# Pooled and local attention before a SoLU feed-forward layer: a shorter conversion of the float64 weights, g taken in where w_out is rounded, and the first batch's pooled q and k formed by matmuls, in a new order of the program

## The chip, the core and the metric

The kernel runs on one core of one Trainium2 chip. The metric is the device time of one execution, in microseconds (us). Before the change three runs gave 586.81, 589.69 and 590.03 us, median 589.69.

## What is computed

The inputs are q, k and v of 8 batches, 8 heads, 576 tokens and 64 dimensions in float32, two weight matrices w_in (512 x 1024) and w_out (1024 x 512) in float64, and a vector g. Per batch and head there are two attentions, whose results are added:

```
q_d = q.reshape(B, H, Sd, factor, D).mean(axis=3)      # factor 4; k_d and v_d alike
out_up = np.repeat(sm_attn(q_d, k_d, v_d), factor, axis=2)
mask = np.abs(pos[:, None] - pos[None, :]) < factor
scores = np.where(mask, scale * q @ k.T, -1000000000.0)
out_local = softmax(scores) @ v
x = (out_up + out_local)                               # as 4608 tokens x 512
h = x @ w_in
solu = h * softmax(h)
ln = (solu - mu) / np.sqrt(var + 1e-06) * g_ln
out = ln @ w_out
```

## The kernel before

**Engines.** PE is the matrix engine, DVE, ACT and POOL are the vector, scalar and general engines, and SP starts the transfers. Every engine works through its own queue in order.

**Feed-forward tiles.** There are 36 tiles of 128 tokens. Every operand of the two big products is split into a rounded high part and the rest (`xh`, `xl`; `wi_h`, `wi_l`; `uh`, `ul`; `wo_h`, `wo_l`), and a product takes three matmuls for each piece: 24 matmuls make `h` (L862) and 24 make `o` (L986). `h` has one buffer in PSUM. The next tile's `h` can start only when the DVE has read the last one twice, for its maximum (`nmx`, L870) and for the product h*exp(h) (L877), with ACT's exp (L874) between. The product, centred, goes out to DRAM and comes back as `v`, is transposed by the DVE (L963) and split into `uh` and `ul` for `o`. So a tile's `o` comes several tiles after its `h`.

**Weights.** The two matrices arrive as 16 pieces of 128 x 512 float64 numbers (0 to 7 of w_in, 8 to 15 of w_out), each seen as pairs of 32-bit words. `f32` makes float32 of a piece in five steps: ACT takes the absolute value of the high word as a float (L364), the DVE or POOL clamps it (L366), the DVE shifts it left by 3 and masks it (L370), the DVE puts sign and top exponent bit in (L375), and the DVE puts the top three bits of the low word in (L379). `piece` then rounds it to the high part on ACT (L410), after a multiplication by g on ACT for w_out (L409), and POOL or the DVE subtracts (L412). All of w_in has to be there before the first `h`.

**Attention of a batch.** For the first two batches (`EarlyBatch`) the tokens lie six to a partition, and PE transposes them: per pair of heads 12 matmuls for q and 12 for k against an identity (L557), into `qp` and `kp` in PSUM, from where ACT or the DVE copies them to `qT` and `kT` (L263 and L265). The DVE then adds groups of four tokens (L419) into `qd_flat` and `kd`. From these come pooled scores (`sd`, L788), their maximum (`mxd`, L795), exp (`pd`, L803), a transpose (`pdt`), and the product with pooled v (`po`). Local attention works on windows of 64 tokens: scores `sc` (L607), for the first two batches on top of a mask added by PE (L600), maximum `mxl` (L620), difference `pl` (L622), exp, sum `sml` (L639), a transpose `plt`, and the product `xp`. Later batches are transposed by the DVE. In the first batch `kp` and the odd `sd` and `sc` use the two banks that later hold `h` (`ps_h`); the others rotate through two buffers (`ps_a`).

**Fillers.** `keep_clock` puts pairs of bfloat16 matmuls whose result nobody reads (`warm`, L1043) on PE, 24 pairs in all.

**The order.** The program is first written down as a list of some 2,000 steps. `ORDER`, a table of step numbers, sets in which order they are given out, and so the order within each engine's queue, SP's transfers among them. `OTHER` lists the steps that use the second of two possible engines. Queues, buffers and semaphores then decide when each runs.

Of the kernel before, what the change touches and what calls it, by code (L numbers as in the profile page):

```python
# [10 lines left out]
F32 = mybir.dt.float32  # L11
F32R = mybir.dt.float32r
I32 = mybir.dt.int32
BF16 = mybir.dt.bfloat16
# [6 lines left out]
F64_LO = struct.unpack("<f", struct.pack("<I", 0x38000000))[0]  # L21
F64_HI = struct.unpack("<f", struct.pack("<I", 0x47EFFFFF))[0]

# [114 lines left out]
def pooled_local_attention_then_solu_ffn(  # L138
# [10 lines left out]
    nc = tc.nc  # L149
# [1006 lines left out]
```

## Time and profile before

The profiled execution took 585.0 us itself, 583.2 us of it from its first to its last instruction (the span). That is below all three timed runs.

| | before |
|---|---|
| time, median of 3 runs | 589.69 us (586.81 to 590.03) |
| profiled execution, own time | 585.0 us |
| its span | 583.2 us |
| TensorE clock granted | 0.999 |
| ACT busy | 333.8 us (57%) |
| POOL busy | 299.5 us (51%) |

The profile gives for each engine the time in which it had an instruction running. A matmul's record reaches to its modelled end, so a row of dependent short matmuls looks busy although PE does little in it; the starts of instructions tell more there. In rows of the timeline the first number is the start in us from the span's beginning, the second the length of the stretch, the word after it the engine, then line, operation, output and inputs, shape and count. A bracket gives idle time of the engine ahead of it and who ended it.

### The profile page before, as it was taken

The numbers are of one execution on the slowest core, as the hardware profiler recorded it, in microseconds if no ns is written. First come the engines' busy times: TensorE is split into PE (matmuls) and PEld (weight loads), VectorE is DVE, ScalarE is ACT, GpSimd is POOL, SyncE is SP. The second block draws the span as 40 slices with busy tenths as digits, with TensorE's granted clock in tenths as the row PEclk, the third lists the DMA queues.
The fourth block names the chain that finished last, engine by engine and source line by source line (L and its number), as shares of the span: only waits on it lengthen the run. The fifth ranks groups of instructions, "written<-read, shape, count | busy, mean of one in ns | idle before, by whom it ended". The sixth has DMA issues, their size and how long they took to land.

```text
span 583.2 us, 15261 instructions
## 1 busy us (share of the span) xinstructions
PE 564.1 (97%) x5852; PEld 434.1 (74%) x5852; DVE 469.3 (80%) x779; ACT 333.8 (57%) x750; POOL 299.5 (51%) x447
## 2 busy tenths in 40 slices
PE   7899998999999999999999999999999999999996
PEld 3676666777787777877777777777787777788875
DVE  7989999898988879998977967899878877545541
ACT  4778678468546646565565753466445654444442
POOL 3657677957454745648533546356433752334120
PEclk9999999999999999999999999999999999999999
DMA  8997767787877888876867976766755145304230
GB/s 280 286 213 187 189 148 193 200 193 171 228 160 185 188 191 169 194 198 157 208 153 195 228 190 167 212 157 159 195 163 148 56 145 164 127 36 163 90 110 37
DMA packets 207113, 99.59 MB, mean 171 GB/s; under 512 B 163136, under 2 KB 193344, under 8 KB 207040
## 3 DMA queue, kind: packets, MB, share of 16 engines
q1 hardware_dynamic: 207040, 98.61, 66.3%
q8 instruction: 46, 0.75, 0.6%
q14 instruction: 27, 0.22, 0.1%
HBM read 65.54 MB, written 27.79 MB: 160 GB/s over the span
## 4 chain that ended last, share of the span: by engine, by line
PE 64%; DVE 14%; SPq 7%; DMA 5%; ACT 4%; issue 3%; POOL 2%; POOLq 0%; DVEq 0%
PE o L986 27%; PE h L862 25%; SPq L286 4%; DMA v<-u 3%; PE po L844 2%; PE sd L788 2%; PE xp L753 1%; PE pdt L823 1%; PE sc L607 1%; PE sc L695 1%; DVE w L375 1%; DVE qd_flat L419 1%; DVE nmx L870 1%; SPq L942 1%; DVE e L877 1%
## 5 line engine op out<-in xcount | busy, mean ns | idle before, releaser
L986 PE MATMUL o<-wo_h,uh 128*128 128x512 f32 x288 | 116.6, 405 | 1.5 <-ACT osb L993 0.8
L862 PE MATMUL h<-wi_h,xh 128*128 128x512 f32 x288 | 116.9, 406 | 0.8 <-DVE e L877 0.6
L862 PE MATMUL h<-wi_h,xl 128*128 128x512 f32 x288 | 114.1, 396 | 0.7 <-POOL xl L1020 0.7
L986 PE MATMUL o<-wo_l,uh 128*128 128x512 f32 x288 | 113.8, 395 | 0.0
L862 PE MATMUL h<-wi_l,xh 128*128 128x512 f32 x288 | 113.7, 395 | 0.0
L986 PE MATMUL o<-wo_h,ul 128*128 128x512 f32 x288 | 78.9, 395 | 0.0
L972 POOL TENSOR_TENSOR ul<-v,uh 128x512 fp32r<-128x512 f32 x40 | 51.9, 1297 | 42.8 <-ACT uh L969 41.6
L874 ACT ACTIVATE e<-h,nmx 128x1024 f32<-128x1024 f32 x36 | 40.2, 1116 | 49.1 <-DVE nmx L870 45.5
L986 PEld LDWEIGHTS o<-wo_h,uh 128*128 128x128 f32 x288 | 54.0, 188 | 16.8 <-ACT osb L993 1.5
L862 PEld LDWEIGHTS h<-wi_h,xh 128*128 128x128 f32 x288 | 54.1, 188 | 15.8 <-issue 2.9
L862 PEld LDWEIGHTS h<-wi_h,xl 128*128 128x128 f32 x288 | 54.1, 188 | 15.4 <-POOL xl L1020 2.1
L986 PEld LDWEIGHTS o<-wo_h,ul 128*128 128x128 f32 x288 | 54.0, 188 | 13.4 <-DVE ul L972 0.3
L870 DVE TENSOR_REDUCE nmx<-h 128x1 f32<-128x1024 f32 x36 | 43.8, 1216 | 24.2 <-PE h L862 24.2
L986 PEld LDWEIGHTS o<-wo_l,uh 128*128 128x128 f32 x288 | 54.1, 188 | 12.0
L862 PEld LDWEIGHTS h<-wi_l,xh 128*128 128x128 f32 x288 | 54.1, 188 | 11.9
L877 DVE SCALAR_TENSOR_TENSOR e<-h,e 128x1024 f32<-128x1024 f32 x36 | 43.8, 1217 | 14.2 <-ACT e L874 14.0
L969 ACT ACTIVATE uh<-v 128x512 fp32r<-128x512 f32 x70 | 42.9, 624 | 18.5 <-issue 7.1
L963 DVE STREAM_TRANSPOSE v<-v 128x512 f32<-128x512 f32 x70 | 46.4, 689 | 7.6 <-DMA v<-u 7.5
L993 ACT ACTIVATE osb<-o,s 128x512 f32<-128x512 f32 x36 | 24.6, 682 | 40.0 <-PE o L986 22.1
L1020 POOL TENSOR_TENSOR xl<-x,xh 128x512 fp32r<-128x512 f32 (+1 forms) x26 | 32.9, 1268 | 22.5 <-ACT xh L1017 22.2
L487 POOL TENSOR_TENSOR vs<-vs 72x512 f32<-72x512 f32 x24 | 31.9, 1328 | 17.5 <-DMA vs<-in_v_dram 9.0
L882 POOL TENSOR_SCALAR nmu<-su 128x1 f32<-128x1 f32 x36 | 8.1, 226 | 60.1 <-DVE e L877 57.2
(128 smaller groups left out, 1116.3 us busy)
## 6 DMA issues: line engine op xcount, KB each, us to landing
u<-e SPq DMA_DIRECT2D x35, 512.0 KB
v<-u SPq DMA_DIRECT2D x140, 128.0 KB
vs<-in_v_dram SPq DMA_DIRECT2D x32, 288.0 KB
out_dram<-osb SPq DMA_DIRECT2D x36, 256.0 KB
qm<-in_q_dram SPq DMA_DIRECT2D x96, 72.0 KB
km<-in_k_dram SPq DMA_DIRECT2D x96, 72.0 KB
vw<-in_v_dram SPq DMA_DIRECT2D x80, 64.0 KB
vw<-in_v_dram SPq DMA_DIRECT2D x40, 128.0 KB
```

What stands on the lines that cost most here:

```text
L286: nc.sync.dma_start(t[nm][Q * 32:Q * 32 + 32, pr], src[b, 2 * pr + par, :, dh * 32:dh * 32 + 32].rearrange("(k t) d -> t k d", t=32),)
L487: eng.tensor_tensor(out=vs[:, :, 0:2 * D], in0=vs[:, :, 0:2 * D], in1=vs[:, :, 2 * D:4 * D], op=ALU.add)
L862: nc.tensor.matmul(hps[:, n, :], src[:, cc, :], wt[:, cc, n * 512:(n + 1) * 512], start=(cc == 0 and src is xh and wt is wi_h), stop=(cc = ...
L870: nc.vector.tensor_reduce(out=nmx, in_=hf, op=ALU.max, axis=AX.X, negate=True)
L874: nc.scalar.activation(e, hf, AF.Exp, bias=nmx, scale=1.0, accum_out=se)
L877: nc.vector.scalar_tensor_tensor(out=e, in0=hf, scalar=1.0, in1=e, op0=ALU.mult, op1=ALU.mult, accum_out=su)
L963: nc.vector.transpose(vg, vg)
L969: nc.scalar.activation(uh, tp, AF.Copy)
L972: (usual if v is None else engine(usual, nc.vector)).tensor_tensor(out=ul, in0=tp, in1=uh.bitcast(F32), op=ALU.subtract)
L986: nc.tensor.matmul(o, src[:, j, :], wt[:, 4 * g + j, :], start=(g == 0 and j == 0 and src is uh and wt is wo_h), stop=(g == 1 and j == 3 a ...
L993: nc.scalar.activation(osb, o, AF.Copy, scale=s)
L1020: engine(nc.gpsimd, nc.vector).tensor_tensor(out=l, in0=src, in1=h.bitcast(F32), op=ALU.subtract)
```

## The change

Four things change together.

1. `f32` has a shorter chain. The absolute value is scaled by a power of two while ACT reads it, so the clamp needs no mask after it. The low word's top three bits are made either by ACT, from the word's top byte with a scale, or by the DVE with a shift. A DVE operation on single bytes puts the inverted sign beside them, and one last DVE operation shifts the high part by 3 and combines. On the DVE stand always two operations (a one-source one on bytes, L376 in the new file, and a two-source one, L382), and the clamp (L365) or the shift (L372) where they are not on POOL or ACT.
2. `G_LATE` is set: for w_out ACT multiplies by g and rounds in one operation (L404 in the new file), and the DVE makes the low part from the unscaled piece in one operation (L406), where POOL had done a subtraction.
3. For batch 0 the sums of four tokens are made by PE: beside each group of 12 transposes stand 14 matmuls (L575) that add into the same PSUM buffer behind the transposed tokens, from where a second, small copy takes them (128 x 144). The eight DVE sums of batch 0 are gone.
4. `ORDER` and `OTHER` are new throughout.

```
     WARM = 24
     SUMS_ON_PE = 0
-    G_LATE = False
+    G_LATE = True
     FIRST_ON_PE = ()
+    POOLED_ON_PE = 1
...
         def f32(self, n):
             hl = self.raw.pop(n)
             hi, lo = hl[:, :, 1], hl[:, :, 0]
+            by = hl.bitcast(U8).rearrange("p c (two e) -> p c two e", two=2)
+            low = by[:, :, 0, 3]
             w = moe.tile([P, DO], F32, tag="osb", name=f"w32_{n}", bufs=2)
-            nc.scalar.activation(t, hi.bitcast(F32), AF.Abs)
+            nc.scalar.activation(w, hi.bitcast(F32), AF.Abs, scale=2.0 ** -16)
             yield
             engine(nc.vector, nc.gpsimd).tensor_scalar(
-                out=t, in0=t, scalar1=F64_LO, scalar2=F64_HI, op0=ALU.max, op1=ALU.min
-            )
+                out=w, in0=w, scalar1=2.0 ** -31, scalar2=F32_TOP, op0=ALU.max, op1=ALU.min
+            )
+            yield
+            if engine(nc.scalar, nc.vector) is nc.scalar:
+                nc.scalar.activation(lo, low, AF.Copy, scale=7.49 / 255)
+            else:
+                nc.vector.tensor_scalar(
+                    out=lo, in0=lo, scalar1=29, scalar2=None, op0=ALU.logical_shift_right
+                )
             yield
             nc.vector.tensor_scalar(
-                out=ti, in0=ti, scalar1=3, scalar2=0x3FFFFFFF,
-                op0=ALU.logical_shift_left, op1=ALU.bitwise_and,
-            )
-            yield
-            nc.vector.scalar_tensor_tensor(
-                out=ti, in0=hi, scalar=-0x40000000, in1=ti, op0=ALU.bitwise_and, op1=ALU.bitwise_or
-            )
-            yield
+                out=low, in0=by[:, :, 1, 3], scalar1=0x80, scalar2=0x80,
+                op0=ALU.bitwise_and, op1=ALU.bitwise_xor,
+            )
+            yield
+            wi = w.bitcast(I32)
             nc.vector.scalar_tensor_tensor(
-                out=w.bitcast(I32), in0=lo, scalar=29, in1=ti,
-                op0=ALU.logical_shift_right, op1=ALU.bitwise_or
+                out=wi, in0=wi, scalar=3, in1=lo, op0=ALU.logical_shift_left, op1=ALU.bitwise_xor
             )
             return w
...
+                if self.by_pe:
+                    three = tp[:, 0, n:n + SD].rearrange("x (m j) -> x m j", j=3)
+                    turn = ident[0:self.TP, 0:self.TP].rearrange("p (m e) -> p m e", e=2)
+                    for at_t, (t, js, es) in enumerate((
+                        (0, (0, 2, 1), (0, 2)), (1, (0, 2, 1), (0, 2)),
+                        (2, (2, 3, 1), (1, 2)), (2, (0, 1, 1), (0, 1)), (3, (0, 3, 2), (0, 2)),
+                        (4, (1, 3, 1), (0, 2)), (5, (1, 3, 1), (0, 2)),
+                    )):
+                        for par in range(2):
+                            nc.tensor.matmul(
+                                three[rows(par), :, js[0]:js[1]:js[2]],
+                                self.qk[nm, pr][:, par, t],
+                                turn[:, :, es[0]:es[1]], start=at_t == 0, stop=at_t == 6,
+                            )
...
+                if self.by_pe:
+                    copy(
+                        engine(nc.scalar, nc.vector),
+                        self.qd[pr] if nm == "q" else self.kd[:, pr], tp[:, 0, n:n + SD],
+                    )
+                yield
+            if self.by_pe:
+                return
...
-            row(bt.pair_steps(pr), 6 if bt.b < EARLY else 4)
+            row(bt.pair_steps(pr), 6 if POOLED_ON_PE <= bt.b < EARLY else 4)
...
-7 192 160 6 193 194 24 195 196 197 161 162 25 163 164 8 165 198 199 166 168 167 169 170 176 12
+14 24 16 9 26 27 25 28 29 168 30 169 170 171 172 31 32 173 174 33 34 175 176 177 35 56 152 2 57
```

What the new order does is seen in three places of the queues. SP's queue used to begin with a piece of w_in, another piece, then q and k; it now begins with q and k of the first pair, then a piece. PE used to have seven pairs of fillers ahead of its first transposes and has three.

PE's queue at the first batch's second pair of heads, before the change (`qp` and `kp` are the transposes of q and k, `sd` the pooled scores):

```order
L557 MATMUL qp_1_229<-ident,qm_141 64x96 x12
L557 MATMUL kp_245<-ident,km_142 64x96 x12
L788 MATMUL sd_0_260<-kd_220,qd_flat 64x144 x6
L557 MATMUL qp_2_271<-ident,qm_141 64x96 x12
L557 MATMUL kp_289<-ident,km_142 64x96 x12
```

The same place of PE's queue with the change:

```order
L575 MATMUL qp_1_211<-ident,qm_131 64x48x2 x6
L561 MATMUL kp_242<-ident,km_132 64x96 x12
L575 MATMUL kp_242<-ident,km_132 64x48x2 x4
L575 MATMUL kp_242<-ident,km_132 64x48 x4
L575 MATMUL kp_242<-ident,km_132 64x48x2 x6
L813 MATMUL sd_0_276<-kd_200,qd_flat 64x144 x6
```

Each transpose group of batch 0 is followed by 14 sums, ten of 96 columns and four of 48, ahead of everything that comes after it on PE.

The DVE's queue near its start, before (`w_1`, `w_2` are pieces of w_in, `stage` holds a loaded piece, `qd_flat` and `kd` are the pooled q and k):

```order
L375 SCALAR_TENSOR_TENSOR w_1_162<-stage,w_1_162 128x512
L419 TENSOR_REDUCE qd_flat<-qT_185 128x144
L419 TENSOR_REDUCE kd_220<-kT_186 128x144
L379 SCALAR_TENSOR_TENSOR w_1_162<-stage,w_1_162 128x512
L370 TENSOR_SCALAR w_2_172<-w_2_172 128x512
L375 SCALAR_TENSOR_TENSOR w_2_172<-w_2_165,w_2_172 128x512
L379 SCALAR_TENSOR_TENSOR w_2_172<-w_2_165,w_2_172 128x512
L795 TENSOR_REDUCE mxd_0_267<-sd_0_260 128x3
```

The DVE's first rows after its preparations, with the change:

```order
L264 COPY kT_141<-kp_172 128x576
L264 COPY kd_200<-kp_172 128x144
L372 TENSOR_SCALAR w_2_202<-w_2_202 128x512
L376 TENSOR_SCALAR w_2_202<-w_2_202 128x512
L382 SCALAR_TENSOR_TENSOR w_2_205<-w_2_205,w_2_202 128x512
L820 TENSOR_REDUCE mxd_0_288<-sd_0_276 128x3
L372 TENSOR_SCALAR w_3_270<-w_3_270 128x512
L365 TENSOR_SCALAR w_0_297<-w_0_297 128x512
```

The DVE no longer begins with weights: its first row waits for PE's second transpose group. A piece takes two to four of its rows (as the clamp and the low bits are put), where it took three or four.

PE's queue at the fourth feed-forward tile (`h_1639` before, `h_1704` with the change), before:

```order
L986 MATMUL o_1589<-wo_l,uh_0_1503 128x512
L986 MATMUL o_1589<-wo_h,ul_0_1504 128x512 x4
L655 MATMUL plt_2_1627<-ident,pl_110 128x128 x4
L862 MATMUL h_1639<-wi_h,xh_1511 128x512
L862 MATMUL h_1639<-wi_l,xh_1511 128x512
L862 MATMUL h_1639<-wi_h,xl_1512 128x512
```

The rows behind that tile's last matmul, with the change:

```order
L887 MATMUL h_1704<-wi_h,xl_1547 128x512
L680 MATMUL plt_4_1741<-ident,pl_108 128x128 x4
L690 MATMUL xp_2_1757<-plT_2_1729,vw_2_1751 64x58 x16
L632 MATMUL sc_1_1777<-kT_1370,qT_1589 64x64 x16
L690 MATMUL xp_1_1811<-plT_1_1638,vw_1_1010 64x58 x16
L690 MATMUL xp_4_1830<-plT_4_1794,vw_4_1798 64x56 x16
L869 MATMUL po_0_1859<-pdT_0_1505,vd_1360 64x144 x4
L632 MATMUL sc_3_1867<-kT_1370,qT_1589 64x64 x16
L632 MATMUL sc_0_1887<-kT_1370,qT_1589 64x64 x16
L869 MATMUL po_1_1906<-pdT_1_1588,vd_1360 64x144 x4
L848 MATMUL pdt_2_1917<-ident,pd_2_975 72x64 x12
L632 MATMUL sc_2_1936<-kT_1370,qT_1589 64x64 x16
```

The first half of the first tile's `o`, 12 matmuls, stood ahead of the fourth tile's `h`; it now stands behind it and behind these rows. All other rows that had been done at the fourth `h` have been done there in both orders. By the fifth `h` both orders have done the same work, except one `plt` that the new order has not, and one pair of fillers that it puts later.

More of the change, by code (lines that the diff above doesn't have):

```diff
@@ L1 @@
+import struct
 import math
-import struct
 from contextlib import ExitStack
@@ L13 @@
 I32 = mybir.dt.int32
+U8 = mybir.dt.uint8
+F32_TOP = struct.unpack("<f", struct.pack("<I", 0x3FEFFFFF))[0]
 BF16 = mybir.dt.bfloat16
@@ L18 @@
 PSUM = bass.MemoryType.PSUM
-F64_LO = struct.unpack("<f", struct.pack("<I", 0x38000000))[0]
-F64_HI = struct.unpack("<f", struct.pack("<I", 0x47EFFFFF))[0]
 ORDER = """
[96 rows of a table removed]
[95 rows of a table added]
 """
 OTHER = """
[7 rows of a table removed]
[7 rows of a table added]
 """
@@ L360, in f32 @@
             hi, lo = hl[:, :, 1], hl[:, :, 0]
+            by = hl.bitcast(U8).rearrange("p c (two e) -> p c two e", two=2)
+            low = by[:, :, 0, 3]
             w = moe.tile([P, DO], F32, tag="osb", name=f"w32_{n}", bufs=2)
-            t = w
-            ti = t.bitcast(I32)
-            nc.scalar.activation(t, hi.bitcast(F32), AF.Abs)
+            nc.scalar.activation(w, hi.bitcast(F32), AF.Abs, scale=2.0 ** -16)
             yield
             engine(nc.vector, nc.gpsimd).tensor_scalar(
-                out=t, in0=t, scalar1=F64_LO, scalar2=F64_HI, op0=ALU.max, op1=ALU.min
+                out=w, in0=w, scalar1=2.0 ** -31, scalar2=F32_TOP, op0=ALU.max, op1=ALU.min
             )
             yield
+            if engine(nc.scalar, nc.vector) is nc.scalar:
[5 more added lines that the diff above has]
+            yield
             nc.vector.tensor_scalar(
-                out=ti, in0=ti, scalar1=3, scalar2=0x3FFFFFFF,
-                op0=ALU.logical_shift_left, op1=ALU.bitwise_and,
+                out=low, in0=by[:, :, 1, 3], scalar1=0x80, scalar2=0x80,
+                op0=ALU.bitwise_and, op1=ALU.bitwise_xor,
             )
             yield
+            wi = w.bitcast(I32)
             nc.vector.scalar_tensor_tensor(
-                out=ti, in0=hi, scalar=-0x40000000, in1=ti, op0=ALU.bitwise_and, op1=ALU.bitwise_or
-            )
-            yield
-            nc.vector.scalar_tensor_tensor(
-                out=w.bitcast(I32), in0=lo, scalar=29, in1=ti,
-                op0=ALU.logical_shift_right, op1=ALU.bitwise_or
+                out=wi, in0=wi, scalar=3, in1=lo, op0=ALU.logical_shift_left, op1=ALU.bitwise_xor
             )
@@ L525, in pooled_local_attention_then_solu_ffn @@
         TP = S // TT
+        by_pe = property(lambda self: self.b < POOLED_ON_PE)
         def room(self):
```

203 rows, old and new, of tables (ORDER, OTHER) are left out of this document.

## The prediction

> **What bounds the kernel now.** First the page: busy shares, and the chain of work that ended last by engine.
>
> ```profile
> PE 564.1 (97%) x5852; PEld 434.1 (74%) x5852; DVE 469.3 (80%) x779; ACT 333.8 (57%) x750; POOL 299.5 (51%) x447
> PE 64%; DVE 14%; SPq 7%; DMA 5%; ACT 4%; issue 3%; POOL 2%; POOLq 0%; DVEq 0%
> ```
>
> PE leads, but its records reach to modelled ends, so the second view is the table of windows, cut at the first local scores (24.2), the first `h` (57.3), the end of the fifth `h` (124.5) and the last tiles (565). After the colon stand the window's length and the busy time of PE, PEld, DVE, ACT and POOL.
>
> ```profile
> 0.00:24.20 24.20, 19.27 (x250) 11.46 (x251) 20.13 (x40) 14.22 (x34) 10.55 (x16) 1.00 0.95 285
> 24.20:57.30 33.10, 29.56 (x649) 21.73 (x647) 30.37 (x61) 26.44 (x72) 22.78 (x22) 1.00 0.89 205
> 57.30:124.50 67.20, 64.58 (x841) 48.29 (x837) 64.54 (x111) 47.83 (x100) 51.70 (x59) 1.00 0.76 189
> 124.50:565.00 440.50, 437.80 (x4065) 342.95 (x4064) 351.00 (x566) 239.83 (x538) 213.38 (x349) 1.00 0.65 164
> 565.00:583.20 18.20, 12.84 (x57) 9.70 (x56) 3.23 (x5) 5.45 (x9) 1.12 (x4) 0.96 0.12 44
> ```
>
> From 124.5 to 565 PE idles 440.50 - 437.80 = 2.7 us: there only less PE work would help, and the change takes none away. From 24.2 to 124.5 the DVE is busy 94.9 of 100.3 us. So the start is paced by the DVE and by what PE hands it, and the end follows from how early PE has the fifth tile's `h` behind it with the same other work done. The third view is the timeline at the landmarks.
>
> ```profile
> 3.32 6.49 PE L1043 MATMUL warm<-ident_b 128*128 128x512 bf16 x14 [3.32 <-DVE ident_b L216]
> 9.74 1.02 PEld L557 LDWEIGHTS qp<-ident,qm 96*64 96x64 f32 x24 [0.42 <-issue]
> 9.75 1.21 PE L557 MATMUL qp<-ident,qm 96*64 96x96 f32 x24
> 24.20 0.39 PE L600 MATMUL sc<-mask_b,ident_b 128*128 128x256 bf16 x2
> 26.66 0.68 DVE L620 TENSOR_REDUCE mxl<-sc 128x8 f32<-128x512 f32 x1
> 54.63 0.61 DVE L578 TENSOR_TENSOR x<-x,xp 128x464 f32<-128x464 f32 x1
> 57.29 0.50 PE L862 MATMUL h<-wi_h,xh 128*128 128x512 f32 x1
> 91.71 1.19 DVE L877 SCALAR_TENSOR_TENSOR e<-h,e 128x1024 f32<-128x1024 f32 x1
> 93.02 0.48 PE L862 MATMUL h<-wi_h,xh 128*128 128x512 f32 x1
> 118.61 0.59 PE L862 MATMUL h<-wi_h,xh 128*128 128x512 f32 x1
> ```
>
> The rows are: the first fillers, the first transposes with their weight loads, the first scores, their maximum on the DVE, the second addition into x (after it tile 0 can be split), the first `h`, the third tile's L877, and the fourth and fifth `h`. The fourth `h` starts 0.1 us after that L877 ends (91.71 + 1.19 = 92.9): the DVE sets it. From there to the fifth `h` PE has work without a gap, 118.61 - 93.02 = 25.6 us.
>
> **The change, part by part.** Durations come from groups by tile (minimum, median, maximum in ns) and by line (busy us, mean ns).
>
> ```profile
> L370 DVE TENSOR_SCALAR w<-w x16: 383/424/1886, 5.7 to 98.8; 128x512 int32<-128x512 int32 x16
> L375 DVE SCALAR_TENSOR_TENSOR w<-w,w x12: 647/687/693, 6.1 to 99.2; 128x512 int32<-128x512 int32 x12
> L366 DVE TENSOR_SCALAR w<-w x10: 375/420/1025, 5.2 to 95.5; 128x512 f32<-128x512 f32 x10
> L366 POOL TENSOR_SCALAR w<-w x6: 1905/1954/2436, 12.7 to 96.7; 128x512 f32<-128x512 f32 x6
> L419 DVE TENSOR_REDUCE kd<-kT 128x144 f32<-128x576 f32 x32 | 23.3, 735 | 0.1
> L263 ACT ACTIVATE pdT<-pdt 72x288 f32<-72x288 f32 x49 | 18.3, 401 | 30.0 <-PE pdt L823 22.9 <-DVE pdT L265 4.9 <-PE po L844 2.2
> L409 ACT ACTIVATE w<-w,g_sb 128x512 f32<-128x512 f32 x8 | 5.8, 723 | 3.7 <-DVE w L379 3.7
> L410 ACT ACTIVATE wo_h<-w 128x512 fp32r<-128x512 f32 x8 | 5.1, 632 | 0.3
> ```
>
> *Conversion.* Before, a piece costs the DVE 0.42 (clamp) + 0.42 + 0.69 + 0.69 = 2.22 us, after 0.42 (clamp) + x + 0.69, where x is the byte operation. The trace has none on bytes. Its bounds are the one-source row (0.42) and the two-source row (0.69); I take 0.42, as it has one source and stands nearest to L370. That is 0.7 us off a piece, 11 us in all. The low bits on ACT (12 of 16) cost some 0.65 each, as L410; taking g in while rounding saves L409, 0.72, eight times. ACT, at 26.4 of 33.1 us, hides it. The DVE gets w_out's eight subtractions from POOL (0.69 each), 5.5 us back.
>
> [...]
>
> *Sums on PE.* Each of batch 0's eight groups gets 10 matmuls of 96 columns and 4 of 48, 10 x 96 + 4 x 48 = 1152 columns, as many as its 12 transposes (12 x 96). Those take 24 passes in 0.98 us (the weight loads 1.02 less the tail). So I add 1.0 us a group, 8.0 in all. Bounds: 28 passes at the weight loads' 42 ns give 1.19; at the scores' rate (a row follows) 28 x 21.6 ns = 0.6. The DVE loses eight sums (8 x 0.66 start to start, 5.3 us) and takes with ACT eight small copies, 0.3 us each (below the 72x288 row's 0.40).
>
> *Up to the first scores.* The new order has q and k loaded first and three filler pairs in place of seven ahead of the transposes. A filler takes (9.75 - 3.32)/14 = 0.46 us, so PE starts the transposes at 3.32 + 6 x 0.46 = 6.1. From there the old order took 24.20 - 9.75 = 14.45; the new adds 8.0, leaves out one filler pair of four (0.55) and puts one `pdt` (0.47) ahead: 6.1 + 14.45 + 8.0 - 0.55 + 0.47 = 28.5, which is **4.3 us later**. The eight sums that the DVE loses lie in this stretch, where it now waits for PE: they buy nothing.
>
> *From there to the first `h`.* The old DVE needed 26.66 to 55.16 (start of the next row) for 51 rows. Of these 28.5 us it idled 2.28.
>
> ```profile
> 29.06 0.69 DVE L620 TENSOR_REDUCE mxl<-sc 128x8 f32<-128x512 f32 x1 [0.39 <-PE sc L607]
> 36.21 0.61 DVE L795 TENSOR_REDUCE mxd<-sd 128x3 f32<-128x432 f32 x1 [1.08 <-PE sd L788]
> 41.97 0.45 DVE L265 COPY pdT<-pdt 72x288 f32<-72x288 f32 x1 [0.81 <-ACT pdT L263]
> 25.83 0.69 PE L607 MATMUL sc<-kT,qT 64*64 64x64 f32 x32
> ```
>
> So 26.2 us of work. The new queue has 52 rows from the first maximum to the split of tile 0, which it also does itself (0.65; POOL took 1.29 before). Against the old ones: 1.0 us less of conversion; three more rows on local scores (1.9), two more sums of batch 1 (1.3), two rows for pooled v (1.0) and a larger copy (0.3); five rows less for a sum, a maximum and reciprocals (1.6). That is 1.9 us more, 28.1 in all. It starts when the first scores are made, 28.5 + 0.9 (mask 0.3, 32 passes 0.69): done at 57.5, the first `h` at 57.6, level with 57.29. That leaves the DVE no idle time; with all of the old, it is 59.9.
>
> *To the fourth `h`.* The old DVE took 55.16 to 92.9, 37.7 us, without idling. The new queue has 57 rows for 60: five pieces' steps against five (3.9 us less), four subtractions of w_out (2.6 more), and a few rows less, together 1.7 us less. It starts 2.3 later (57.5) and reaches the fourth `h` at 93.5 + 0.1, **0.5 us later** than 93.02.
>
> *To the fifth `h`.* The half of the first `o` that stood ahead of the fourth `h` now stands behind it: 12 matmuls of 0.233 us, **2.8 us more** for PE in a stretch without gaps. One filler pair (0.55) goes to a later place, where I take it to fill a gap. Later only the order differs; the DVE carries less (11 + 5.3 - 5.5 = 11 us of 469), and I take 1.0 off PE's 2.7 us of idle time there. The last tiles stand in both orders alike.
>
> **Sum:** 0.5 + 2.8 - 0.55 - 1.0 = +1.7 us (1.75 rounded down). The profiled execution took 585.0 us itself (583.2 of span, the rest around it), which the change makes 586.7. That profile lies 0.8% below the median of the runs, 589.69. The same 1.7 us on the median give **591.4 us**.
>
> **The rivals.** *Slower: the byte operation costs as much as a two-source one.* Nine of them stand between the first scores and the fourth `h`, on the engine that paces this stretch: 9 x (0.69 - 0.42) = 2.4 us, so +4.1. It decides as soon as the mean of the new line is over 0.5 us. L370's maximum of 1886 ns, against a median of 424, speaks for it: one-source operations of the DVE are already held up at times, as is POOL's clamp (1954 ns for what the DVE does in 420), and the change gives POOL nine clamps for six. One or two more such delays of 1.46 us end at +5 to +7. I price it at +5: **594.7**. Against it stand L370 and L366 at 0.42.
>
> [...]
>
> *Faster: the sums on PE cost little.* If they run at the scores' rate, 0.6 us a group and not 1.0, the first scores come 3.2 us earlier. If PE's waits in the old first stretch (14.45 less 8 x 0.98, three `sd` of 0.63 and four filler pairs of 0.55: 2.5 us) swallow the rest, up to 5.7 earlier. The DVE then starts as much earlier and everything up to the fifth `h` moves along: +1.7 - 3.2 = -1.5, or -4.0. I price it at -4.0: **585.7**. For it: the DVE loses 11 us of work and is the engine on the chain. Against it: the transposes, of the same shape, show 42 ns a pass.
>
> *The order elsewhere.* Between 124.5 and 565 the new table can win at most 2.7 us, and lose, at the idle share of the window before (2.62 of 67.2, 3.9%), 17. It decides when PE's idle time there exceeds 5 us. I price it at +5.7: **595.4**.
>
> **How the numbers follow.** Forecast 0.42 (of it 0.32 within 0.5%, 0.06 faster, 0.04 slower), slower rival 0.22 (0.20 slower, 0.02 within), faster rival 0.24 (0.20 faster, 0.04 within), the order elsewhere 0.12 (0.09 slower, 0.03 within). That is 0.26 faster by over 0.5%, 0.41 within, 0.33 slower; 0.5% is 2.9 us, about what a measurement of this kernel can tell from no change. The range reaches below the faster rival to where all of its 5.7 us and the 1.0 come through (584.5) and above the slower one to its +7 with idle time as before in the second stretch, some 2 us (598.5).
>
> **What will show it.** In the changed kernel's profile the first transposes should start near 6.1, the first scores near 28.5, the first `h` near 57.6, the fourth near 93.6 and the fifth near 121 (25.6 + 2.8 - 0.55 later, less one `plt` of 0.5 that comes behind it). The byte operation (L376) should have a median near 420 ns, a sum group on PE should last 1.0 us, and PE should idle about 2 us between the fifth `h` and 565. I am wrong if the first scores come before 26, if the byte operation takes 0.6 us or more, or if the stretch after the fifth `h` changes by more than 3 us.

## The result, and the profile after

The changed kernel takes 605.19 us, median of 4 runs (602.77 to 606.85), against 589.36 us of the kernel before on the same chip: ratio 1.0298, 95% interval 1.024 to 1.0355, slower. The forecast was 591.4 us with a range of 584.5 to 598.5, so the time lies outside the range. The profiled execution took 605.95 us itself (span 604.2), where the sum had given 586.7.

First the landmarks, taken from the timeline. The last one is the 36th tile's `nmx`.

| from | to | forecast | before | after | after less forecast |
|---|---|---|---|---|---|
| start | first scores | 28.5 | 24.20 | 31.84 | +3.3 |
| first scores | first `h` | 29.1 | 33.09 | 37.96 | +8.9 |
| first `h` | fourth `h` | 36.0 | 35.73 | 38.50 | +2.5 |
| fourth `h` | fifth `h` | 27.4 | 25.59 | 30.90 | +3.5 |
| fifth `h` | last `nmx` | 440.05 | 441.05 | 441.36 | +1.3 |

All but 1.3 us of the error arises before the fifth `h`. Next stand the table of windows of the changed kernel, cut at these landmarks (columns as in the prediction), and then the timeline rows of the last `nmx`, of before and of after.

```profile
0.00:31.84 31.84, 25.69 (x477) 20.54 (x477) 16.41 (x35) 13.22 (x38) 11.90 (x17) 1.00 0.94 230
31.84:69.80 37.96, 33.18 (x608) 23.72 (x608) 29.10 (x53) 25.08 (x64) 16.39 (x16) 0.87 0.70 168
69.80:108.30 38.50, 33.45 (x445) 23.49 (x443) 38.01 (x61) 27.36 (x60) 27.60 (x25) 1.00 0.78 182
108.30:139.20 30.90, 28.51 (x402) 22.27 (x401) 27.41 (x47) 18.77 (x38) 18.48 (x26) 0.94 0.69 166
139.20:580.56 441.36, 439.04 (x4072) 344.07 (x4071) 347.78 (x558) 245.33 (x551) 221.70 (x355) 1.00 0.63 164
```

```profile
559.66 1.22 DVE L870 TENSOR_REDUCE nmx<-h 128x1 f32<-128x1024 f32 x1 [4.03 <-PE h L862]
```

```profile
580.56 1.23 DVE L895 TENSOR_REDUCE nmx<-h 128x1 f32<-128x1024 f32 x1 [3.54 <-PE h L887]
```

From 31.84 to 69.80 the DVE works 29.1 us, 1.0 more than the forecast's 28.1, but it stands idle 8.9 us. In the same row the granted clock is 0.87. The timeline of PE in the changed kernel says why ("issue" in a bracket means that no semaphore in the profile ended the wait):

```profile
6.42 2.19 PE L561 MATMUL qp<-ident,qm 96*64 96x96 f32 x24
8.40 1.57 PE L575 MATMUL qp<-ident,qm 96*64 96x96 f32 x28
9.80 1.16 PE L561 MATMUL kp<-ident,km 96*64 96x96 f32 x24
10.79 1.23 PE L575 MATMUL kp<-ident,km 96*64 96x96 f32 x28
11.85 1.16 PE L561 MATMUL qp<-ident,qm 96*64 96x96 f32 x24
...
17.79 0.46 PE L813 MATMUL sd<-kd,qd_flat 64*64 64x144 f32 x4 [1.27 <-issue]
...
31.84 0.39 PE L625 MATMUL sc<-mask_b,ident_b 128*128 128x256 bf16 x2 [0.75 <-ACT kd L262]
...
39.95 0.69 PE L632 MATMUL sc<-kT,qT 64*64 64x64 f32 x10 [3.94 <-issue]
...
44.30 2.19 PE L561 MATMUL qp<-ident,qm 96*64 96x96 f32 x24
...
50.68 1.21 PE L561 MATMUL qp<-ident,qm 96*64 96x96 f32 x24
...
121.01 0.38 PE L632 MATMUL sc<-kT,qT 64*64 64x64 f32 x9 [1.52 <-issue]
```

Ahead of 39.95 PE stands for 3.94 us in the middle of one score tile, after 22 of its 32 matmuls, and no semaphore is named. Then the same 24 transposes take 2.19 us at 44.30 and 1.21 us at 50.68. Windows of the changed kernel show the clock (before the DMA share) of the wait, of the time behind it, and then of the wait of 1.52 us and the time behind that one:

```profile
36.00:39.95 3.95, 0.01 (x3) 0.01 (x1) 1.01 (x2) 0.95 (x2) 2.44 (x3) 0.98 0.98 216
39.95:50.00 10.05, 10.05 (x107) 6.56 (x108) 6.02 (x11) 3.51 (x7) 1.04 (x1) 0.50 0.68 178
50.00:60.00 10.00, 10.00 (x197) 8.26 (x198) 9.37 (x19) 9.34 (x25) 5.06 (x5) 1.00 0.20 34
119.50:121.00 1.50, 0.00 (x0) 0.00 (x0) 1.09 (x2) 1.50 (x4) 1.42 (x3) 1.00 0.64 178
121.75:125.15 3.40, 3.40 (x53) 2.57 (x50) 2.25 (x6) 1.55 (x3) 1.93 (x2) 0.50 0.48 124
```

In the trace's clock record the clock is a half from 39.82 to 50.06 us (10.24 us) and from 121.74 to 125.15 (3.41 us). The record begins only at 9.10 us; the windows count the time ahead of it as full clock.

**What PE waited for.** Number PE's records (weight loads, matmuls, semaphores) in order from 0. The first instruction after each wait "issue" is number 449, 1217 and 3521 after the change (17.79, 39.95, 121.01 us), and 705 and 961 before it (28.69, 35.84 us). All of these leave 193 when divided by 256. One of the two rows of the kernel before (the other stands with e14_before_vw below):

```profile
28.69 0.33 PE L607 MATMUL sc<-kT,qT 64*64 64x64 f32 x4 [1.15 <-issue]
```

The DMA view has a queue of instructions whose packets are 16 KB each: 48 of them in the changed kernel, whose PE has 12,300 records, and 46 before the change, with 11,868, so 256 and 258 records to a packet. For two stretches of the changed kernel, 31.83 to 37.2 us and then 37.2 to 38.6, it lists (packets, MB, share):

```profile
q1 hardware_dynamic: 1033, 1.32, 105.9%
...
q1 hardware_dynamic: 541, 0.23, 84.0%
q8 instruction: 1, 0.02, 5.7%
```

PE reaches number 961, and so a new block of 256, at 31.83. The one packet of the next block begins at 37.28, ends at 38.56, and PE goes on at 39.95. Between 31.83 and 37.28 the DMA engines are full with data (105.9% in the list up to 37.2). At all five waits PE goes on 1.3 to 1.7 us after such a packet has landed. While the DMA share is near 1 (1.01 from 11.2 to 39.95 us in the changed kernel, 1.04 from 25 to 40 before the change), a packet begins 2.9 to 5.5 us after PE's entry into the block ahead; from 50 us on (0.70 up to 130 in the changed kernel) mostly within 2 us. So up to 8.1 us pass from PE's entry into one block (31.83) until the next one can be used (39.95; at the other four waits 5.1 to 7.2 us pass), and the stretch of four score tiles uses a block up in 4.2 us.

That these packets bring PE its instructions, 256 at a time, is read from these numbers and times; no row of the profile names it.

Last the groups of the new operations on the DVE in the changed kernel (minimum, median, maximum in ns):

```profile
L376 DVE TENSOR_SCALAR w<-w x12: 720/756/1739, 13.8 to 126.7; 128x512 uint8<-128x512 uint8 x12
L406 DVE SCALAR_TENSOR_TENSOR wo_l<-w,g_sb,wo_h x8: 720/748/2171, 75.6 to 129.0; 128x512 fp32r<-128x512 f32 x8
```

The byte operation takes 0.756 us, above both bounds of the prediction (0.42 and 0.69).

### The profile page after: what moved, and what is told of

It is laid out like the page before. It is cut to its first block, busy times and chain, and to the rows that moved or that the text cites. A ratio compares the mean times of both kernels' runs of the same rounds, so it can differ in the third digit from the quotient of the medians.

```text
span 604.2 us, 15665 instructions
## 1 busy us (share of the span) xinstructions
PE 578.0 (96%) x6076; PEld 448.0 (74%) x6076; DVE 465.3 (77%) x761; ACT 337.6 (56%) x760; POOL 299.3 (50%) x447
## 4 chain that ended last, share of the span: by engine, by line
PE 76%; DVE 10%; SPq 3%; issue 3%; ACT 3%; DMA 3%; POOL 2%; DVEq 0%; ACTq 0%; POOLq 0%
PE o L1011 30%; PE h L887 28%; PE po L869 3%; PE sd L813 2%; SPq L285 2%; PE xp L778 2%; PE pdt L848 2%; PE sc L632 2%; PE sc L720 1%; PE plt L680 1%; PE xp L690 1%; PE warm L1068 1%; DMA vs<-in_v_dram 1%; DMA qm<-in_q_dram 1%; PE qp L561 1%
## 5 line engine op out<-in xcount | busy, mean ns | idle before, releaser
L997 POOL TENSOR_TENSOR ul<-v,uh 128x512 fp32r<-128x512 f32 x37 | 50.1, 1360 | 32.9 <-PE o L1011 19.1
L907 POOL TENSOR_SCALAR nmu<-su 128x1 f32<-128x1 f32 x36 | 9.4, 262 | 75.0 <-DVE e L902 74.9
L1045 POOL TENSOR_TENSOR xl<-x,xh 128x512 fp32r<-128x512 f32 (+1 forms) x25 | 31.6, 1266 | 27.1 <-ACT xh L1042 26.7
L944 ACT ACTIVATE e<-e 128x1024 f32<-128x1024 f32 x35 | 36.8, 1050 | 4.0 <-DMA u<-e 3.7
L489 POOL TENSOR_TENSOR vs<-vs 72x512 f32<-72x512 f32 x26 | 36.7, 1411 | 1.7 <-DMA vs<-in_v_dram 1.4
```

What stands on the lines that cost most here:

```text
L489: eng.tensor_tensor(out=vs[:, :, 0:2 * D], in0=vs[:, :, 0:2 * D], in1=vs[:, :, 2 * D:4 * D], op=ALU.add)
L944: nc.scalar.activation(e0, e, AF.Square, accum_out=m2)
L997: (usual if v is None else engine(usual, nc.vector)).tensor_tensor(out=ul, in0=tp, in1=uh.bitcast(F32), op=ALU.subtract)
L1045: engine(nc.gpsimd, nc.vector).tensor_tensor(out=l, in0=src, in1=h.bitcast(F32), op=ALU.subtract)
```

## The experiments

All ratios are to the kernel before, run on the same chip beside the experiment. Labels are those that the expectations use.

**One part undone or done alone.** `e1_sums_dve`: in the changed kernel the DVE makes batch 0's sums again.

```
-    POOLED_ON_PE = 1
+    POOLED_ON_PE = 0
```

(the two DVE sums of each pair come into the order right behind its k copy)

> The changed kernel with one part undone: the sums of batch 0 are made by the DVE again, two right behind each pair's k copy; conversion, G_LATE and the new order stay. It takes 448 instructions (224 weight loads, 224 matmuls) off PE's queue. Theory S (supply): PE gets its instructions in blocks of 256, and while transfers fill the DMA engines a block takes 7 us or more, so the changed kernel's PE ran dry (1.27 us at 16.5, 3.94 us at 36.0) and its clock fell to a half for 10.2 us. It expects no wait of PE marked issue over 2 us before the first h, a clock of 1.00 from 24 to 60, the first h at 57 to 61 (69.8 with the sums on PE), and 590 to 596 us. Rival W (work): the sums' 8 us of PE time are what was lost, stalls or not: the first h at about 62, and 596 to 599 us. Rival T (transfers): the new order brings w_in and later q and k too late: the first h stays within 2 us of 69.8, and the time at 603 to 607.

598.2 us, ratio 1.0215 (1.0162 to 1.0268); first `h` at 62.9. Time and first `h` are rival W's. But the clock was not full: PE now stood 3.09 us for a sum of the DVE (until 16.39), and from 17.1 to 27.3 the clock was halved, so this run alone doesn't decide. Without the sums on PE the first `h` comes 6.9 us sooner; undoing them doesn't bring the kernel before back.

`e2_pe_sums`: the kernel before with `POOLED_ON_PE = 1` and L575's matmuls alone.

> The kernel before with one part of the change alone: the sums of batch 0 on PE; old conversion, old order. Theory S: the 448 added instructions make PE run dry while the transfers fill the DMA engines: waits of PE marked issue before 60 us of 4 us or more in sum (2.3 in the kernel before), each at an instruction number that leaves 192 or 193 when divided by 256, the first h 6 to 13 us after 57.3, and 595 to 602 us. Rival W: 8 us of PE work less what PE's waits and the DVE's saved sums swallow: first h 2 to 5 us later, 590 to 594 us. Rival T: the old order's transfers stay as they were: no more than 1 us later, 588 to 591.

595.4 us, 1.0176 (1.0128 to 1.0223), first `h` at 66.7 (+9.4): both as theory S had it, but mostly not by its mechanism. The first scores come at 31.21 (+7.0): PE works almost without pause up to there, so its 8 us of sums come through nearly whole: rival W's mechanism, at more than W's price. Theory S adds one wait "issue" of 1.49 us at 38.59, not the 4 us expected, and 6.8 us of half clock behind it.

`e3_conv`: the kernel before with the new `f32` and `G_LATE = True`. `e4_cut`: the kernel before with

```
+            for c in range(4):
+                nc.tensor.matmul(o[:, c * 128:c * 128 + 128], filler, filler[:, 0:128], ...)
```

in place of each filler matmul of 512 columns.

> The kernel before with the two weight parts alone: the new conversion (low bits always on ACT) and G_LATE; old order, sums on the DVE. The byte operation took a median of 0.756 us in the changed kernel, not 0.42, so a piece saves the DVE 0.36 us and not 0.7 (5.8 us over 16 pieces), and w_out's eight subtractions cost it 8 x 0.75 = 6.0 us. By this the DVE, which paces the stretch up to the fourth h, gains some 2.5 us up to there: 586 to 589 us. Rival: POOL holds the DVE up (maxima of 1.74 us for the byte operation, 2.17 us for the w_out subtraction): 590 to 594 us.

599.4 us, 1.0232 (1.0175 to 1.0289): slower than either guess; e6_f32 and e7_glate below part the two.

> The kernel before with each filler matmul of 512 columns cut into four of 128: the same columns, and no result depends on them; 156 more instructions for PE by 30 us and 288 in all. Theory S: more instructions with the same work cost time wherever supply paces PE: 156 of 256 of a block of 7 us, up to 4 us, so 590.5 to 595 us and the first h 1.5 to 5 us later, with more waits marked issue before 60 us than 2.3. Rival W: the same PE work, so the same time: 588.5 to 590, first h within 1 us of 57.3.

588.83 us, 1.0073 (1.0039 to 1.0107), with the first `h` at 57.0: rival W's time and landmark, where theory S had the first `h` 1.5 to 5 us later and more waits. PE stood once for instructions, 1.31 us at 32.2, again at a number that leaves 193, where the kernel before stood twice. So here the added instructions did not delay the first `h` (57.0 against 57.29): theory S can hold only where a block is used up faster than the next one comes. The 0.7% doesn't arise ahead of the first `h`; in the profile, 444.4 us pass from the fifth `h` to the last `nmx` (441.05 before), and why stays open.

`e5_order`: the kernel before in the new `ORDER` and `OTHER`. `e6_f32`: with the new `f32` alone. `e7_glate`: with `G_LATE = True` alone.

> The kernel before with the new order and the new choice of engines alone: old conversion, g apart, sums of batch 0 by the DVE, two right behind each pair's k copy. The new order with conversion and G_LATE (e1_sums_dve) cost 2.15% against the kernel before, the two weight parts in the old order (e3_conv) 2.3%. Theory O: the order itself costs, since it loads w_in's pieces later and puts fillers where PE doesn't wait (half clock for 10.2 us after a wait of 3.1 us at 16 us in e1_sums_dve): 593 to 600 us where the kernel before takes 585.5, that is 1.3% to 2.5%. Theory V: the weight parts cost wherever they stand, the order is not worse: within 0.5% of the kernel before.

611.4 us, 1.0439 (1.0374 to 1.0505): theory O, and by more than its price. Up to 130 us its profile has no wait "issue" of note, but the clock is a half for 37.6 us, in five stretches, behind waits of PE for the DVE, ACT and POOL of 1.3 to 3.1 us.

> The kernel before with the new conversion alone: low bits always on ACT, old order, g apart. The two weight parts together cost 2.3%; in that profile the DVE waited for ACT's low bits (2.3 us) and for ACT's rounding before w_out's subtraction (3.0 us), and stood idle 11.1 us between the first and the fifth h where it had stood 2.6. Theory F: the conversion carries the loss, because its byte operation has to wait for ACT in the middle of the DVE's chain and ACT has 10.7 us more to do: 1.3% to 2.3% slower. Theory G: G_LATE carries it, because the DVE then waits for ACT's rounding in place of POOL: this one within 0.6% of the kernel before, and e7_glate 1.3% or more slower. In between: both about 1%.

593.24 us, 1.0118 (1.0074 to 1.0162).

> The kernel before with G_LATE alone: old conversion, old order. Theory G: 1.3% to 2.3% slower, waits of the DVE for wo_h of 2.5 us or more. Theory F: within 0.6%, the eight operations that POOL loses and the DVE gains (8 x 0.75 = 6.0 us) being hidden or worth up to 3 us.

598.68 us, 1.0209 (1.0158 to 1.0259). Of the two theories neither holds alone: G_LATE costs what theory G said, but the conversion costs too, more than the 0.6% that theory G allowed it. Every part alone is slower, and the four together (1.0298) cost less than the order alone: the new order with the two weight parts (e1) stands at 1.0215, without them at 1.0439. This suggests that what a part costs by itself is largely what an order made for other lengths makes of it; no run tests that alone. The wait lists up to 130 us of e6_f32 (DVE, first two rows) and of the whole of e7_glate (PE, first row) show how:

```profile
DVE w L379 <- ACT w L373: 6.9, 4, 3.0
DVE stage L379 <- ACT stage L373: 2.7, 2, 2.2
```

```profile
PE sc L607 <- DVE qT L467: 4.7, 1, 4.7
```

With the low bits on ACT the DVE waits 9.6 us for them; with w_out's subtraction on the DVE, PE waits 4.7 us for a transpose queued behind it on the DVE (until 113.40), and the clock is halved for 6.8 us from 112.5.

**The wait for instructions.** `e8_vw_late`: in the changed kernel's `ORDER` step 96 (the load of a window of v) moves from behind step 388 to just ahead of step 411. `e13_vw_mid`: to behind step 404.

> The changed kernel with one load moved: the window of v that SP issues from 31.8 us on, four transfers of 64 KB in small packets, goes some 12 us later in SP's queue; nothing else changes. In the changed kernel PE entered its block of instructions at 31.83, the next block's transfer began at 37.28 and ended at 38.56, and PE stood until 39.95. Theory S: that transfer waited behind data, those four transfers above all; without them it begins 1.2 us or more sooner, PE's wait at the same matmul falls from 3.9 us to 2.7 or less, and the first h comes 1.5 to 9 us sooner (9 if the clock is no longer halved): 1.5% to 2.8% above the kernel before, where the changed kernel stood 3.0% above. Rival: the wait is for something else than instructions, and stays at 3.5 to 4.5 us, with the time where it was.

> The changed kernel with the same load of v moved by less: four transfers from 31.8 us to about 40, behind the loads of the next batch's last q and its fourth window. In e8_vw_late they came so late that a product waited 2.04 us for them, but PE's wait for instructions in the fourth score tile had fallen from 3.94 to 0.40 us. Theory S: the transfer of instructions again begins within 4.5 us of PE's entry into its block (5.45 in the changed kernel), the wait in the score tile is under 1.5 us, no product waits over 1 us for this window, and from the first scores to the first h it takes 30.5 to 32.5 us (38.0 in the changed kernel, 33.5 in e8_vw_late); time 1.5% to 2.8% above the kernel before. Rival: what is left of the 38.0 us is the DVE's own queue: 33 us or more again.

Timeline rows of PE, of e8_vw_late and then of e13_vw_mid:

```profile
36.82 0.44 PE L628 MATMUL sc<-kT,qT 64*64 64x64 f32 x10 [0.40 <-issue]
...
58.17 1.49 PE L686 MATMUL xp<-plT,vw 64*64 64x58 f32 x32 [2.04 <-DMA vw<-in_v_dram]
...
65.78 0.49 PE L883 MATMUL h<-wi_h,xh 128*128 128x512 f32 x1
```

```profile
38.59 0.69 PE L628 MATMUL sc<-kT,qT 64*64 64x64 f32 x10 [3.45 <-issue]
```

In e8_vw_late the wait fell to 0.40 us with the first `h` 4.0 us sooner, as theory S had it. In e13_vw_mid it came back: other data took the load's place, the instructions' packet began 4.82 us after PE's entry, and the first `h` came at 68.3; of theory S's terms for this run none came. Neither run changed the median time measurably: 1.0303 (1.0235 to 1.0371) and 1.0291 (1.0236 to 1.0347), where theory S had 1.5% to 2.8%. In the profiled execution of e8_vw_late the last `nmx` comes at 575.91, 4.65 us sooner than in the changed kernel's, but its four times reach from 601.06 to 608.51 us. Half clocks of 3.4 us stand there at 19.3, 60.3, 101.2 and 118.3 us. The four times of e13_vw_mid warn against putting all on the clock: the execution with a mean granted clock of 0.997 took 605.04 us, the one with 0.983 took 605.67.

`e14_before_vw`: in the kernel before, step 450 (a load of v for batch 1) moves behind step 104.

> The kernel before with one load moved: a window of v of batch 1, four transfers that SP issued from 25.1 us on, goes some 14 us later in its queue. PE's wait for instructions at 28.69 us (1.15 us, a block whose transfer began 3.8 us after PE's entry into the one ahead) stands right behind them. Theory S: that wait falls under 0.6 us, and the time by 0 to 2 us, 0.3% at most, since the DVE paces this stretch. Rival: the data were not what the instructions waited for: the wait stays over 1 us and the time within 0.2%.

1.0022 (0.9987 to 1.0056), no difference. The wait at 28.69 fell from 1.15 to 0.60 us, but the next one grew from 1.13 to 1.95, and this profile shows by itself what such a wait did here. First PE's timeline and a window of e14_before_vw, then both of the kernel before at the same place:

```profile
36.18 0.33 PE L783 MATMUL sd<-kd,qd_flat 64*64 64x144 f32 x1 [1.95 <-issue]
...
40.19 2.13 PE L552 MATMUL kp<-ident,km 96*64 96x96 f32 x24
```

```profile
38.10:48.30 10.20, 10.20 (x119) 9.33 (x118) 7.81 (x16) 6.39 (x18) 4.30 (x5) 0.50 0.66 158
```

```profile
35.84 0.33 PE L788 MATMUL sd<-kd,qd_flat 64*64 64x144 f32 x1 [1.13 <-issue]
...
38.87 1.16 PE L557 MATMUL kp<-ident,km 96*64 96x96 f32 x24
```

```profile
38.10:48.30 10.20, 9.79 (x188) 7.41 (x184) 9.25 (x19) 10.11 (x26) 6.20 (x6) 1.00 0.74 167
```

The first `h` comes at 61.02 (before 57.29, +3.7) and the last `nmx` at 563.20 (+3.5): the loss is carried to the end unchanged. The half clock doesn't come in every execution: the mean granted clock of this kernel's 12 runs lies between 0.988 and 0.999, their times between 584.03 and 591.24 us. The kernel before itself, in its 17 runs beside these, goes with the clock: the seven with a mean of 0.998 or more have a median of 583.95 us, the three with 0.990 or less 590.46.

**The DVE's mis-sized terms.** `e9_word`: in the changed kernel

```
-                out=low, in0=by[:, :, 1, 3], scalar1=0x80, scalar2=0x80,
+                out=lo, in0=hi, scalar1=-0x80000000, scalar2=-0x80000000,
```

`e10_g_pool`: `G_LATE = False` in the changed kernel. `e11_both`: both.

> The changed kernel with its byte operation (mean 0.876 us, 16 times) put in place by one operation of the same kind on 32-bit words, as the shift that took 0.42 us; it leaves out the low three bits of every weight. The DVE loses 16 x (0.876 - 0.42) = 7 us of work by 127 us. If that mis-sized term makes the loss (theory D, the DVE paces up to the last weights), the fifth h comes 4 to 7 us sooner than 139.2 and the time is 1.8% to 2.3% above the kernel before, where the changed kernel stood 3.0% above. If PE's instruction supply and its clock make it (theory S), the fifth h comes 0 to 2 us sooner and the time stays 2.6% to 3.2% above; PE still stands over 3 us in the same four score tiles near 36 to 40 us.

> The changed kernel with G_LATE undone: g by an ACT operation of its own, w_out's eight subtractions on POOL as before the change. The DVE loses 8 x 0.75 to 1.03 = 6 to 8 us between 75 and 130 us. Theory D: the stretch from the first to the fifth h (69.4 us in the changed kernel) shortens by 3 to 6 us, and the time is 2.0% to 2.5% above the kernel before. Theory S: the stretch keeps 67 us or more, and the time 2.6% to 3.2% above.

> Both of these at once in the changed kernel (the word operation, which leaves out the low three bits, and G_LATE undone): 13 to 15 us less for the DVE by 130 us. Theory D: 1.0% to 1.8% above the kernel before. Theory S: 2.4% to 3.0% above, since what PE loses before the first h (first scores at 31.8, first h at 69.8) is not touched.

1.0167 (1.0066 to 1.0268), 1.0245 (1.0165 to 1.0325) and 1.0254 (1.0179 to 1.0329). From the first to the fifth `h` they take 66.7, 68.5 and 68.9 us (changed kernel 69.4): 0.5 to 2.7 us less, where theory D had 3 to 6 for e10_g_pool. Theory D's landmark for e9_word came all the same: its fifth `h` is at 132.80, 6.4 us sooner. But 3.7 of these lie ahead of the first scores (28.18), where the DVE waits for PE, and most of the 3.7 is not the edit: PE's first transposes and sums ran 1.2 us faster, and PE stood 0.9 and 0.6 us less at numbers 449 and 961. The times are less clear: e9's interval holds both theories, e10's ratio is theory D's, e11's, with both edits, theory S's. In e9_word and e11_both PE again stood in the score tiles, 4.44 and 3.21 us; in e10_g_pool 1.40.

`e12_fill`: e1_sums_dve with five more filler pairs ahead of the second pooled scores.

> The changed kernel with the sums on the DVE (e1_sums_dve) and five more filler pairs, which do nothing for the result, ahead of the second pooled score tile, where PE stood 3.09 us for a sum of the DVE and the clock was then halved from 17.1 to 27.3 us. Theory C (the clock falls because PE stood, and that is what costs): the five pairs fill 2.3 us of that wait, the half clock at 17 us is gone, the first scores come 3 to 5 us sooner than 29.5, the first h 2 to 5 us sooner than 62.9, and the time is 1.3% to 1.8% above the kernel before where e1_sums_dve stood 2.15% above. If the clock falls for another reason, or its fall is hidden by the DVE: first h within 1 us of 62.9, and 2% to 2.5% above.

596.77 us, 1.0146 (1.0071 to 1.0222), against e1's 1.0215 with overlapping intervals: inconclusive. The half clock at 17 us was gone, but PE then waited 1.02 and 1.50 us for ACT at 20 and 23 us, and it came from 22.5 to 32.7; first scores 1.4 us later, first `h` 1.1 sooner.

## Why the prediction was wrong

**The step that failed** is "That leaves the DVE no idle time": the price of 29.1 us from the first scores to the first `h`. PE was taken to keep the DVE fed, and PE's supply of instructions was not in the sum. The table splits this stretch for each profile in the new order with the sums on PE: its length, PE's waits "issue" in it, half the time at half clock (what a PE that never pauses loses), and what is left.

| kernel | first scores to first `h` | waits "issue" | half of half-clock time | rest |
|---|---|---|---|---|
| changed | 38.0 | 3.9 | 5.1 | 28.9 |
| e13_vw_mid | 37.3 | 3.4 | 5.1 | 28.7 |
| e9_word | 38.0 | 4.4 | 5.1 | 28.4 |
| e11_both | 35.4 | 3.2 | 3.4 | 28.8 |
| e10_g_pool | 34.0 | 1.4 | 3.4 | 29.2 |
| e8_vw_late | 33.5 | 0.4 | 1.7 | 31.4 |

The last row's rest holds the 2.04 us for its moved load; without it 29.4. So 29.1 was about the right price for the work, and what was missing is the wait and the clock: 9.0 us in the changed kernel. That is an upper estimate: the same subtraction leaves 30.8 us for the kernel before (33.09 less 2.28) and 29.2 for e14_before_vw (36.88 less 2.55 and 5.12), which differ in one load, so it can take off some 1.6 us too much. Each row is one execution.

- *Up to the first scores* (+3.3): a sums group takes 1.06 us (from 10.79 to 11.85), where 1.0 was forecast, and e2_pe_sums confirms that they come through. Missing were the wait of 1.27 us at 17.79 and one of 0.75 at 31.84 (number 961; the view names ACT, whose copy had ended 0.5 us before). A third term was a slow start of PE: the first group's transposes and sums took 1.98 and 1.40 us, not 0.99 and 1.06. Up to 9.04 us PE starts four transposes or sums every 0.32 us, as it does at half clock behind 44.30, then about every 0.165, and the clock record begins at 9.10. Other profiles show the same turn where their record begins, at 6.59 (e9_word), 8.29 (before) and 13.02 (e10_g_pool). The prediction took the fillers' 0.46 us as their length, but that mixes both rates: before the change, seven pairs of fillers covered the slow start, and three no longer do, which cost (9.10 - 6.42)/2 = 1.3 us.
- *First to fourth `h`* (+2.5): the DVE was busy 38.0 of 38.5 us, as the prediction had it paced, but with 2 us more work: the byte operation was mis-sized (0.756, mean 0.876, not 0.42), as was w_out's subtraction (mean 1.03, not 0.69). Six DVE operations took 4.3 us more in all than the medians of their groups, each while POOL had an instruction running; before the change three took 2.2 us more, again while POOL had one. That POOL held them up, no run shows. One of w_out's eight subtractions had stood on the DVE already (L412, 0.684 us at 53.9), so the change moved seven. With the byte operation and w_out's subtraction taken away (e11_both) the stretch still took 38.1 us, 1.7 of it lost to a half clock, with the DVE idle 5.6 us. How much of the 2.5 us is DVE work stays open.
- *Fourth to fifth `h`* (+3.5): the 2.8 us of products behind the fourth `h` were right. 30.9 less the wait of 1.52 us at 121.01 and the 1.7 us of half clock behind it is 27.7, against 27.4.
- *After the fifth `h`*: PE idles 2.3 us, forecast 2, and the end follows the fifth `h` as the prediction said; the 1.0 us taken off for less DVE work didn't come.

Waits for instructions and the half clocks behind them make at most 2.0 + 9.0 + 3.2 = 14.3 us (rounded terms) of the 19.3 us by which the sum failed, and the slow start 1.3.

**The rivals.** The slower one met its own condition (a mean of L376 over 0.5 us), and of the prediction's three signs of being wrong this one came (0.6 us or more); but at 0.5 to 2.7 us its mechanism is not what made most of the time. The faster one fell: the sums cost 1.06 us a group. The order elsewhere didn't decide: the long stretch took 441.4 us against 441.05. No rival had PE run dry, though the profile before showed it: two waits "issue" of 1.15 and 1.13 us between the first scores and the first `h`, with the DMA share at 1.00 and more from 25 to 40 us. By its own terms the range runs from 584.7 to 598.7 us, not from 584.5 to 598.5; 605.19 lies outside either.

## What to carry to other kernels

Count the instructions that a change adds to an engine, not only their work, and set them against the transfers that run beside them: in the changed kernel PE used up 256 short ones in 4.2 us (31.83 to 36.0), and the next 256 could be used only 8.1 us after that start, at a DMA share of 1.01 from 31.83 to 39.95. A wait of PE can cost more than its own length: behind the 1.95 us in e14_before_vw stood 10.2 us of half clock, the first `h` came 3.7 us later, and of this loss ahead of the bound stretch 3.5 us were still there at the last `nmx`. In a program whose order was made for its lengths, each part of a change alone may lose (here 1.2% to 4.4%) without saying what the parts are worth together.

## What the hardware showed that was not expected

- The half clock came for 3.4 us (changed kernel at 121.74), 6.8 (e7_glate at 112.5) or 10.2 (changed kernel at 39.82), and after waits of PE as short as 1.29 us (e13_vw_mid at 92.22), 1.37 (e10_g_pool at 116.91) and 1.52 (changed kernel at 121.01). After those of 1.15 and 1.13 us in the kernel before it did not come, but neither did it after 1.29 us at 93.78 and 1.98 at 105.31 in the changed kernel. So the length of one wait does not decide. The lengths are one, two and three times 3.4 us; what decides, these runs do not show.

```profile
105.31 0.69 PE L690 MATMUL xp<-plT,vw 64*64 64x58 f32 x32 [1.98 <-ACT pdT L262]
```

- A DVE operation with one source on single bytes, eight bytes apart, takes 0.756 us for 512 of them, where e9_word's on 32-bit words, also eight bytes apart, takes 0.422. The row of its group:

```profile
L376 DVE TENSOR_SCALAR w<-w x12: 385/422/754, 12.6 to 121.0; 128x512 int32<-128x512 int32 x12
```
